# An accumulating DMA in the weight conversion, seven products for the last step of the first pair, and weights made in pairs

## The chip, the cores and the metric

The kernel runs on one NeuronCore of a Trainium2 chip, and the metric is the time of one execution on the device in microseconds (us). TensorE (PE) multiplies matrices, VectorE (DVE) and ScalarE (ACT) work element by element, GpSimd (POOL) and SyncE (SP) issue most of the DMAs. Every engine works through its own list of instructions in order; semaphores hold an instruction back until what it needs is there.

## The reference

An attention over channels and then two feed-forward layers, all in float32, with N = 6016 tokens, C = 256 channels and 2048 hidden features:

```python
qn = q / (np.linalg.norm(q, axis=1, keepdims=True) + 1e-06)   # q, k, v: (1, 6016, 256)
kn = k / (np.linalg.norm(k, axis=1, keepdims=True) + 1e-06)
s = kn.transpose(0, 2, 1) @ qn / tau                          # (256, 256)
s = s - s.max(-1, keepdims=True)
a = np.exp(s); a /= a.sum(-1, keepdims=True) + 1e-09
x = (v @ a).reshape(6016, 256)
h = x @ w_in                                                  # layer 1: 256 -> 2048
x = (h * (1.0 / (1.0 + np.exp(-1.702 * h)))) @ w_out          #          2048 -> 256
h = x @ w_in2                                                 # layer 2
x = (np.maximum(h, 0.0) + alpha * np.minimum(h, 0.0)) @ w_out2
```

The second layer's weights and alpha are inputs of their own (written w_in2, w_out2 here).

## The kernel before, in words

**Three passes for one product.** A float32 operand is held as two float32r values, hi (rounded) and lo (the rest), and a product is three matmuls: hi x hi, hi x lo, lo x hi (PASSES). The weights come as 64-bit numbers and must be turned into such pairs on the chip (class Convert, L103 to L171).

**The attention is folded into the weights.** The 256 x 256 matrix a is never applied to the tokens. For layer 1 the kernel multiplies it into w_in: for each group of 256 hidden features (j = 0 to 7) `make_w` (L480) runs 12 matmuls of 256 columns into the PSUM tile pw, and `keep_hi` on ACT (L492) and `keep_lo` on DVE (L496) store W of that j in the SBUF tile wi.

**Tiles.** Tokens go in 12 chunks (10 of 512 columns, 2 of 448), two to a pair, so 6 pairs a layer. For one pair and one j, the hidden block has 2 x 2 parts (two features groups f, two chunks c). The first pair of layer 1 forms each part directly (`direct`, L770): 4 units of two products, 24 matmuls, and beside them the 24 output matmuls (`Outs`, L699) of the j before. All other pairs use `quartet` (L792): a Winograd form with 7 products in place of 8, 21 matmuls, whose operands are sums of token blocks (T1 to T4, made by `prepare`, L542) and sums of weight blocks (S1 to S4, made by `combine`, L591). A unit is: ACT applies the activation (act, g), ACT makes its hi part (ghi), DVE its lo part (glo).

**Conversion.** A piece is 512 columns of w_in (ia[j], "inner") or w_out (ob_[j], "outer"); j = 4, 5 and 6, 7 are double pieces of 1024. Each piece is loaded by SP into one of two raw buffers (L125), scaled on ACT (scale, p, L130), and then taken through six DVE steps: shift (L133), signed (L137), power (L147), rest (L150), less (L166) and low (L169), with one ACT copy (hi, L143) between signed and less. The next raw load may start when rest has freed a buffer.

**Order.** The lists are written out by hand (manual_schedule) and filled by a small planner: after each unit `beside` (L641) first runs the put-off ACT instructions (`put_off`, in the order in which they were put off) and then as many conversion steps and background steps (`bg`) as fit into an allowance (FIRST = 2.1 us a unit in the first pair, plus up to 1.0 left over), by listed costs. `conv.need(pieces)` forces the steps until the pieces are made. In the first pair, unit 1 (the second) of each j calls `emit_w(j + 1)`, which needs ia[j + 1]; the start of j needs ob_[j - 1].

**Prologue.** PE forms the 256 x 256 product of k and q (gram) while q and k stream in; its last rows are put behind the norms (nrm), and the column factors are spread over the partitions by a small matmul (bc) that ACT copies to rq before the row scores (L458). The exponent (L463), a transpose (pt) and its hi and lo parts (eT) follow, then W of j = 0 and 1.

**End.** The last block of outputs is copied in two halves, each with its own DMA (L715 to L718).

Of the kernel before, what the change touches and what calls it, by code (L numbers as in the profile page):

```python
# [34 lines left out]
TAIL = 12  # L35
ON_VECTOR = (4, 5, 6, 8)
# [20 lines left out]
def attention_then_two_ffns(ctx: ExitStack, tc: tile.TileContext, q, k, vT, tau, w1i, w1o, w2i, w2o, alpha, outT):  # L57
# [45 lines left out]
    class Convert:  # L103
# [4 lines left out]
        most = 2 * PIECE  # L108
        pool = None

        def __init__(self, src, pair, done=None):
            self.src, self.pair, self.done = src, pair, done
            self.made = False
            self.a = src.shape[1]
            self.n = self.a * src.shape[2]
# [11 lines left out]
        def scale(self):  # L127

            self.p = self.tile("p", F32, 2)
            nc.scalar.activation(self.p, f32(self.raw[:, :, 1]), AF.Copy, scale=2.0**-112)  # L130
# [43 lines left out]
    class Converter:  # L174


        STEPS = (("shift", 0.45), ("signed", 0.7), ("power", 0.45), ("rest", 0.7), ("less", 0.7), ("low", 0.7))

        def __init__(self):
            self.todo, self.loaded, self.ready, self.open, self.at = [], [], [], None, 0  # L180

            self.ahead = False
            self.held = 0
# [13 lines left out]

        def cost(self):
            return self.time(self.open or (self.ready + self.loaded + self.todo)[0])

        def time(self, piece):
            t = self.STEPS[self.at][1]
            return 2 * t - 0.15 if piece.n > PIECE else t

        def waits(self):

            if not self.open:
# [5 lines left out]
        def needs(self):  # L213
            return [self.ready[0].scale] if self.at == 0 else [self.open.copy] if self.at == 4 else []

        def step(self):

            if self.waits():
                scalar_work()
            if not self.open:  # L220
                self.open = self.ready.pop(0)
                self.held = 1
            do, t = self.STEPS[self.at][0], self.time(self.open)
            getattr(self.open, do)()
            self.at += 1
            if do == "rest":
                self.held = 0
                self.scale()
                if self.ahead:
                    self.load()  # L230
            if self.at == len(self.STEPS):
# [11 lines left out]
        def left(self):  # L243
            return self.todo + self.loaded + self.ready + [x for x in (self.open,) if x]
# [10 lines left out]
    with tc.manual_schedule():  # L255
# [5 lines left out]
        wi_pair = {}  # L261
# [5 lines left out]
        ident = sm.tile([P, P], F32, name="ident")  # L267
        ones = sm.tile([P, P], F32, name="ones")
        ET = tuple(sm.tile([P, 2, 2, P], F32R, name=f"eT_{h}") for h in ("hi", "lo"))

        def inner(j, n=1):
            def pair():
                if j % 2 == 0:
                    t = wi_first.pop() if wi_first else wi_tiles()
# [13 lines left out]
        for made, piece, spans in ((ia, inner, ((0, 1), (1, 1), (2, 1), (3, 1), (4, 2), (6, 2))),  # L288
                                   (ob_, outer, ((0, 1), (1, 1), (2, 1), (3, 1), (4, 2), (6, 2)))):
# [3 lines left out]
        conv.todo = [ia[1], ob_[0], ia[2], ob_[1], ia[3], ob_[2], ia[4], ob_[3], ob_[4], ia[6], ob_[6]]  # L293
# [19 lines left out]
        def operand(pool=None):  # L313
# [3 lines left out]
            slot[0] += 1  # L317
            return xin[i > 3].tile([P, 2, T], F32R, tag=f"x{i}", name="x")
# [12 lines left out]
        with ExitStack() as pre:  # L331
# [96 lines left out]
            conv.steps(2)  # L428
            put_off.pop(0)()
# [13 lines left out]
            rq = sm.tile([P, C], F32, name="rq")  # L443
# [643 lines left out]
```

## Time and profile before

| | before |
|---|---|
| time, median of 3 runs | 1034.97 us (1034.52 to 1034.99) |
| profiled execution | 1034.92 us, span 1033.2 us |
| PE busy | 1027.2 us, 99% of the span |
| DVE busy | 766.1 us, 74% |
| ACT busy | 753.5 us, 73% |
| POOL busy | 31.3 us, 3% |
| granted TensorE clock, mean | 0.999 of full speed |

A profile is one execution. Its span runs from the first to the last recorded instruction; the time of the execution is 1.7 us longer. A busy share is an average over stages, so the rows below also look at single stretches. A row of the timeline begins with the start in us from the span's start and the duration; "[0.3 <-X]" says that the engine was idle for 0.3 us and that X ended it.

### The profile page before, as it was taken

To read this page: it belongs to the slowest core of one execution; us is meant where nothing else is said; L and a number is where in the kernel's file an instruction comes from. 1 tells how busy PE (TensorE), PEld (TensorE's weight loads), DVE (VectorE), ACT (ScalarE), POOL (GpSimd) and SP (SyncE) were. 2 spreads that over 40 slices of the span, in tenths; PEclk is the share of its full clock that TensorE was granted. 3 is DMA by queue.
4 is the path that set the end of the run, shared out by engine and by line. 5 is a ranking of instruction groups with operands and counts; after the bars stand their busy time and mean duration, and the time that the engine had idled before them with its cause. 6 is when DMAs were issued, how large, how long until landed. Compare 5 with 4: busy or idle time off the path is not lost.

```text
span 1033.2 us, 12543 instructions
## 1 busy us (share of the span) xinstructions
PE 1027.2 (99%) x4664; PEld 868.0 (84%) x4664; DVE 766.1 (74%) x1233; ACT 753.5 (73%) x1259; POOL 31.3 (3%) x42
## 2 busy tenths in 40 slices
PE   9999999999999999999999999999999999999998
PEld 8888888888888888888998888888888888888997
DVE  5789977878778787445637777787877787877765
ACT  6776667778777777666767777777777777867776
POOL 4400000000000000000110000000000000000000
PEclk9999999999999999999999999999999999999999
DMA  9635012125224323003543001001001000000101
GB/s 359 242 105 180 1 63 96 41 77 179 77 82 158 99 95 133 0 1 122 204 169 113 1 21 62 1 21 62 0 21 62 1 18 25 35 1 1 42 0 36
DMA packets 30605, 77.62 MB, mean 75 GB/s; under 512 B 3024, under 2 KB 7760, under 8 KB 30288
## 3 DMA queue, kind: packets, MB, share of 16 engines
q1 hardware_dynamic: 28240, 65.29, 18.1%
q0 software_dynamic: 2304, 11.54, 3.3%
q8 instruction: 36, 0.59, 0.2%
q14 instruction: 25, 0.20, 0.1%
HBM read 52.96 MB, written 23.86 MB: 74 GB/s over the span
## 4 chain that ended last, share of the span: by engine, by line
PE 99%; DMA 0%; SPq 0%; issue 0%; ACT 0%; ACTq 0%
PE ps_o L699 50%; PE ps_h L670 44%; PE gram L348 4%; PE pw L484 1%; DMA qk<-in_k 0%; SPq L368 0%; PE nrm L426 0%; PE bc L447 0%; PE pt L472 0%; ACT s L717 0%; ACTq L1083 0%
## 5 line engine op out<-in xcount | busy, mean ns | idle before, releaser
L699 PE MATMUL ps_o<-ghi,wo 128*128 128x512 f32 (+1 forms) x1536 | 562.5, 386 | 0.0
L670 PE MATMUL ps_h<-x,wi 128*128 128x512 f32 (+1 forms) x2040 | 550.7, 386 | 0.0
L670 PEld LDWEIGHTS ps_h<-x,wi 128*128 128x128 f32 x2040 | 382.2, 188 | 71.8 <-DVE wi L496 0.4
L699 PEld LDWEIGHTS ps_o<-ghi,wo 128*128 128x128 f32 x1536 | 288.6, 188 | 53.6
L699 PE MATMUL ps_o<-glo,wo 128*128 128x512 f32 (+1 forms) x768 | 296.5, 386 | 0.0
L737 DVE TENSOR_TENSOR g<-ps_h,s 128x512 f32<-128x512 f32 (+1 forms) x177 | 120.1, 678 | 94.0 <-PE ps_h L670 60.4
L766 DVE SCALAR_TENSOR_TENSOR glo<-g,sign_sb,ghi 128x512 fp32r<-128x512 f32 (+1 forms) x192 | 141.4, 737 | 55.4 <-ACT ghi L760 51.1
L803 ACT COPY s<-ps_h 128x512 f32<-128x512 f32 (+1 forms) x177 | 102.2, 577 | 104.6 <-PE ps_h L670 100.4
L768 DVE TENSOR_TENSOR glo<-g,ghi 128x512 fp32r<-128x512 f32 (+1 forms) x192 | 126.4, 677 | 67.5 <-ACT ghi L762 67.1
L699 PEld LDWEIGHTS ps_o<-glo,wo 128*128 128x128 f32 x768 | 144.3, 188 | 26.9 <-DVE glo L766 0.3
L760 ACT ACTIVATE ghi<-g,sign_sb 128x512 fp32r<-128x512 f32 (+1 forms) x192 | 137.0, 714 | 16.3 <-DVE g L756 10.9
L762 ACT CAST ghi<-g 128x512 fp32r<-128x512 f32 (+1 forms) x192 | 113.2, 611 | 3.6
L748 ACT ACTIVATE g<-ps_h 128x512 f32<-128x512 f32 (+1 forms) x112 | 65.5, 585 | 37.4 <-PE ps_h L670 36.7
L752 ACT ACTIVATE g<-g,sign_sb 128x512 f32<-128x512 f32 (+1 forms) x97 | 69.5, 717 | 29.1 <-DVE g L737 28.6
L756 DVE SCALAR_TENSOR_TENSOR g<-g,slope_sb 128x512 f32<-128x512 f32 (+1 forms) x97 | 71.6, 739 | 16.8 <-ACT g L752 16.6
L756 DVE SCALAR_TENSOR_TENSOR g<-ps_h,slope_sb,g 128x512 f32<-128x512 f32 (+1 forms) x95 | 69.7, 734 | 0.0
L814 ACT COPY ps_h<-ps_h 128x512 f32<-128x512 f32 (+1 forms) x87 | 49.0, 563 | 28.4 <-PE ps_h L670 27.8
L752 ACT ACTIVATE g<-ps_h,sign_sb 128x512 f32<-128x512 f32 (+1 forms) x95 | 64.2, 676 | 2.0 <-PE ps_h L670 0.2
L748 ACT ACTIVATE g<-g 128x512 f32<-128x512 f32 (+1 forms) x80 | 49.8, 623 | 15.5 <-DVE g L737 15.3
L348 PE MATMUL gram<-qk 128*128 128x256 f32 x156 | 34.3, 381 | 1.0 <-DMA qk<-in_k 1.0
L348 PEld LDWEIGHTS gram<-qk 128*128 128x128 f32 x156 | 29.5, 190 | 5.2 <-issue 1.4
L561 DVE TENSOR_TENSOR x<-t,x 128x512 fp32r<-128x512 f32 (+1 forms) x44 | 29.0, 672 | 0.0
(104 smaller groups left out, 504.7 us busy)
## 6 DMA issues: line engine op xcount, KB each, us to landing
wi<-w2i POOLq DMA_DIRECT2D x8, 896.0 KB, 4.9
xraw<-in_vT SPq DMA_DIRECT2D x10, 512.0 KB, 6.1
x<-ob SPq DMA_DIRECT2D x20, 256.0 KB, 2.4
xraw<-x SPq DMA_DIRECT2D x10, 512.0 KB, 3.5
out_T<-ob SPq DMA_DIRECT2D x20, 256.0 KB, 2.1
qk<-in_q SPq DMA_DIRECT2D x9, 512.0 KB, 10.2
qk<-in_k SPq DMA_DIRECT2D x9, 512.0 KB, 10.3
raw<-in_w2i SPq DMA_DIRECT2D x8, 512.0 KB, 4.1
```

The costliest lines, as they stand in the source:

```text
L348: nc.tensor.matmul(gram[m][:, :C], tiles[i][:, 1, r, m * P:(m + 1) * P], tiles[i][:, 0, r, :], start=(t == 0), stop=(t == R - 1))
L670: nc.tensor.matmul(ps[:, :n], WI[:, wq, a, blk], x[:, b, :n], start=(start and i == 0), stop=(stop and i == 2), skip_group_check=True)
L699: nc.tensor.matmul(acc_ps[c][d][:, :n], WO[:, j, a, f, d * P:(d + 1) * P], (hi, lo)[b][:, :n], start=(start and i == 0), stop=(stop and i ...
L737: nc.vector.tensor_tensor(self.src, ps[:, :self.n], s[:, :self.n], ALU.add)
L748: nc.scalar.activation(self.g, self.src, AF.Gelu_apprx_sigmoid)
L752: nc.scalar.activation(self.g, self.src, AF.Copy, scale=sign_sb[:, self.f])
L756: nc.vector.scalar_tensor_tensor(self.g, self.src, slope_sb[:, self.f], self.g, ALU.mult, ALU.max)
L760: nc.scalar.activation(self.hi, self.g, AF.Copy, scale=sign_sb[:, self.f])
L762: nc.scalar.copy(self.hi, self.g)
L766: nc.vector.scalar_tensor_tensor(self.lo, self.g, sign_sb[:, self.f], f32(self.hi), ALU.mult, ALU.subtract)
L768: nc.vector.tensor_tensor(self.lo, self.g, f32(self.hi), ALU.subtract)
L803: nc.scalar.copy(s[:, :n], ps[:, :n])
```

## The change

All of it lies in the prologue, the first pair of layer 1 and its weights, except for the last output copy.

- Pieces of the first layer are all 512 columns wide. Those with j > 1 (inner) and j > 0 (outer) are "added": their steps are shift, settle, signed, power, rest. After rest, `sent` issues a DMA on POOL's queue that adds top into p in SBUF. The ACT copy to hi is put off at the rest of the next piece (`ask`), and `split` (lo = p - hi, one DVE operation) is done in the settle step of a later piece. p has three buffers and top two.
- The last j of the first pair (j = 7, STRASSEN) goes through `quartet`; its sums of tokens are made in j = 4 to 6 and its sums of weights in j = 5 and 6. The two chunks of the next pair are loaded at j = 6 instead of 3.
- W of j = 4, 5 and of 6, 7 is made by `emit_pair`: 12 matmuls of 512 columns for two j.
- In the prologue the first half of gram is copied to SBUF early, the row scores read bc from PSUM, rq is copied later and without tau (which goes into the row factors), and two rows of gram instead of one follow the first transpose. ident, ones and rq share one tile, which with G serves as scratch for the quartet of j = 7. The operand slots are taken in another order.
- The last output block is one copy and one DMA.

```diff
         def signed(self):
-            self.top = self.tile("top", F32, 1)
+            self.top = self.tile("top", F32, 2 if Convert.deep else 1)
             nc.vector.scalar_tensor_tensor(u32(self.top), self.raw[:, :, 1], 0x80000000, u32(self.p),
                                            ALU.bitwise_and, ALU.bitwise_or)
-            self.hi, self.lo = self.pair()
-            put_off.append(self.copy)
+            if not self.added:
+                self.hi, self.lo = self.pair()
+                put_off.append(self.copy)
 
...
         def copy(self):
+            if self.added:
+                self.hi, self.lo = self.pair()
+                self.top = self.p
             nc.scalar.copy(self.hi, self.like(self.top))
...
+
+        def sent(self):
+            nc.gpsimd.dma_start(out=self.p, in_=self.top, accum_op=ALU.add)
+
+        def split(self):
+            nc.vector.tensor_tensor(self.lo, self.like(self.p), f32(self.hi), ALU.subtract)
+            self.made = True
...
         STEPS = (("shift", 0.45), ("signed", 0.7), ("power", 0.45), ("rest", 0.7), ("less", 0.7), ("low", 0.7))
+        ADDED = (("shift", 0.45), ("settle", 0.7), ("signed", 0.7), ("power", 0.45), ("rest", 0.7))
...
+            do, t = self.list(piece)[self.at]
+            return 0 if do == "settle" and not self.landed() else t
+
+        def landed(self):
+            return self.flying and self.flying[0].asked
+
+        def ask(self):
+            if self.flying and not self.flying[0].asked:
+                self.flying[0].asked = True
+                put_off.append(self.flying[0].copy)
...
             if not self.open:
                 self.open = self.ready.pop(0)
                 self.held = 1
-            do, t = self.STEPS[self.at][0], self.time(self.open)
-            getattr(self.open, do)()
+            steps = self.list(self.open)
+            do, t = steps[self.at][0], self.time(self.open)
+            if do != "settle":
+                getattr(self.open, do)()
+            elif self.landed():
+                self.settle()
             self.at += 1
             if do == "rest":
                 self.held = 0
                 self.scale()
+                if self.open.added:
+                    self.ask()
                 if self.ahead:
                     self.load()
-            if self.at == len(self.STEPS):
+            if self.at == len(steps):
+                if self.open.added:
+                    self.open.sent()
+                    self.flying.append(self.open)
                 self.open, self.at = None, 0
             return t
...
-            return Convert(w1i.rearrange("p (a n) -> p a n", a=2)[:, :, j * C:(j + n) * C], pair)
+            return Convert(w1i.rearrange("p (a n) -> p a n", a=2)[:, :, j * C:(j + n) * C], pair, added=j > 1)
...
-            return Convert(w1o[:, j * PIECE:(j + n) * PIECE].rearrange("p (a n) -> p a n", a=1), pair)
+            return Convert(w1o[:, j * PIECE:(j + n) * PIECE].rearrange("p (a n) -> p a n", a=1), pair, added=j > 0)
...
-        conv.todo = [ia[1], ob_[0], ia[2], ob_[1], ia[3], ob_[2], ia[4], ob_[3], ob_[4], ia[6], ob_[6]]
+        conv.todo = [ia[1], ob_[0], ia[2], ob_[1], ia[3], ob_[2], ia[4], ia[5], ob_[3], ob_[4], ia[6], ia[7], ob_[5], ob_[6], ob_[7]]
...
             conv.steps(2)
+            nc.scalar.copy(G[:, 0], gram[0][:, :C])
             put_off.pop(0)()
             conv.steps(2)
...
-            nc.scalar.activation(rq, bc[:, :C], AF.Copy, scale=tau_sb)
-            low(0, 0)
-            high(1, 0)
+            nc.vector.tensor_scalar(rr[:, 2:4], rr[:, 2:4], tau_sb, None, ALU.mult)
...
-            nc.vector.tensor_tensor_reduce(G[:, m], gram[m][:, :C], rq, rr[:, 2 + m:3 + m], -3e38, ALU.mult, ALU.max,
+            nc.vector.tensor_tensor_reduce(G[:, m], *((gram[1][:, :C], rq) if m else (G[:, 0], bc[:, :C])), rr[:, 2 + m:3 + m], -3e38, ALU.mult, ALU.max,
                                            mx[:, m:m + 1])
...
         scores(0)
         exponent(0)
-        emit_gram(range(R - TAIL + 4, R - 1), (1,))
+        nc.scalar.copy(rq, bc[:, :C])
+        high(1, 0)
+        low(0, 0)
+        emit_gram(range(R - TAIL + 4, R - 2), (1,))
         conv.steps(1)
...
+        def emit_pair(j):
+
+            conv.need([ia[j], ia[j + 1]])
+            for m in range(2):
+                pw = psh.tile([P, T], F32, tag="h", name="pw")
+                for n, (a, b, i) in enumerate((a, b, i) for a, b in PASSES for i in range(2)):
+                    nc.tensor.matmul(pw, ET[a][:, m, i], wi_whole[j][b][:, i], start=(n == 0), stop=(n == 5))
+                hi, lo = (WI[:, j:j + 2, h, 2 * m:2 * m + 2] for h in range(2))
+                src = pw.rearrange("p (j a b) -> p j a b", j=2, a=2)
+                nc.scalar.activation(hi, src, AF.Copy, scale=rs[:, m:m + 1])
+                nc.vector.scalar_tensor_tensor(lo, src, rs[:, m:m + 1], f32(hi), ALU.mult, ALU.subtract)
...
-                        for at in (slice(0, n // 2), slice(n // 2, n)):
-                            ob = sp.tile([P, T], F32, tag="s", name="s", bufs=3)
-                            nc.scalar.copy(ob[:, :n // 2], acc_ps[c][d][:, at])
-                            nc.sync.dma_start(dst[:, at], ob[:, :n // 2])
+                        ob = sp.tile([P, T], F32, tag="s", name="s", bufs=3)
+                        nc.scalar.copy(ob[:, :n], acc_ps[c][d][:, :n])
+                        nc.sync.dma_start(dst, ob[:, :n])
...
-                beside(FIRST, convert=True)
+                beside(FIRST, convert=not own_first[0])
...
             def copy(ps):
+                if narrow:
+                    s = small.pop(0)
+                    small.append(s)
+                    nc.scalar.copy(s, ps)
+                    return s
...
             def mid_way(i):
-                if j < NQ - 1 and i == 1:
+                if j < 3 and i == 1:
                     if j == 0:
                         conv.need([ob_[0]])
                     emit_w(j + 1)
+                if j == 3 and i == 1:
+                    emit_pair(4)
+                if j == 5 and i == 1:
+                    emit_pair(6)
+                    own_first[0] = True
+                    combining_of(7)
...
+                if j == 4 and i == 0:
+                    sums0.extend(prepare(0, 0))
+                    bg.extend(sums0)
+                if j == 6 and i == 0:
+                    own_first[0] = False
+                    finish(sums0)
+                    for c in range(2):
+                        load_tokens(0, 2 + c)
+                if j == 6 and i == 2:
+                    pair1.extend(prepare(0, 1))
+                    bg.extend(pair1[0][:3])
+                    combining_of(0)
+                    bg.extend(pair1[0][3:])
+
+            if j < STRASSEN:
+                outs = direct(j, outs, mid_way)
+                continue
+            finish(combined[j])
+            rest = [x for x in pair1[0] if x in bg]
+            for x in rest:
+                bg.remove(x)
+            first(rest + pair1[1])
+            outs = quartet(0, 0, j, outs, carry)
         conv.need(ob_.values())
-        finish(list(bg))
+        finish(combined[0] + pair1[0])
+        steps_late = [x for x in pair1[1] if x in bg]
...
+                if i == 0:
+                    fresh = [n for n in ((1, 2) if j == 0 else (j + 2,)) if n < STRASSEN]
+                    combined.update({n: combine_wi(n) for n in fresh})
+                    first(sum((combined[n] for n in fresh), []))
```

## Rows read from the trace of the kernel before

**Rows 1.** The page: busy time of the engines, and the chain that ended last.
```profile
PE 1027.2 (99%) x4664; PEld 868.0 (84%) x4664; DVE 766.1 (74%) x1233; ACT 753.5 (73%) x1259; POOL 31.3 (3%) x42
...
PE 99%; DMA 0%; SPq 0%; issue 0%; ACT 0%; ACTq 0%
```

**Rows 2.** The chain in order of time: start us, us, what.
```profile
63.29 1.44 PE pw L484 x12
75.64 1.43 PE pw L484 x12
...
213.68 1.36 PE ps_h L670 x6
```

**Rows 3.** Busy time by stretch: us, then each engine's busy us, clock, DMA.
```profile
60.00:90.00 30.00, 30.00 (x151) 25.51 (x150) 28.33 (x47) 20.68 (x36) 0.00 (x0) 1.00 0.39 123
```

**Rows 4.** Timeline of DVE, third inner piece: start, us, line, operation.
```profile
59.75 0.69 DVE L150 SCALAR_TENSOR_TENSOR p<-raw,p 128x512 f32<-128x512 uint32 x1
...
61.75 0.69 DVE L169 TENSOR_TENSOR wi_lo<-top,p 128x512 fp32r<-128x512 f32 x1
62.36 0.42 DVE L133 TENSOR_SCALAR p<-p 128x512 uint32<-128x512 uint32 x1
```

**Rows 5.** Timeline of PE, W of j = 2.
```profile
63.36 0.40 PE L484 MATMUL pw<-wi_lo,eT_hi 128*128 128x256 f32 x2
```

**Rows 6.** Raw loads: one issue, its us to landing, then all from 30 to 110.
```profile
60.51 0.55 SPq L125 DMA_DIRECT2D raw<-in_w1i  x1
...
raw<-in_w1i SPq DMA_DIRECT2D x1, 512.0 KB, 4.3
...
DMA to landing us min/median/max: 3.5/4.8/7.2
```

**Rows 7.** Timeline of ACT beside the third inner piece.
```profile
63.54 0.62 ACT L143 CAST wo<-top 128x512 fp32r<-128x512 f32 x1 [1.90 <-DVE top L137]
...
65.21 0.67 ACT L130 ACTIVATE p<-raw 128x512 f32<-128x512 f32 x1
```

**Rows 8.** DMA issues: queue, count, KB each, median us to landing.
```profile
x<-ob SPq DMA_DIRECT2D x20, 256.0 KB, 2.4
...
qk<-in_k SPq DMA_DIRECT2D x9, 512.0 KB, 10.3
...
wo<-w2o POOLq DMA_DIRECT2D x8, 512.0 KB, 5.5
```

**Rows 9.** Timeline of ACT and PE where the second pair begins.
```profile
128.23 1.13 ACT L557 CAST x<-t 128x512 fp32r<-128x512 f32 x2
...
142.16 0.60 ACT L748 ACTIVATE g<-ps_h 128x512 f32<-128x512 f32 x1 [1.47 <-PE ps_h L670]
142.79 0.62 ACT L762 CAST ghi<-g 128x512 fp32r<-128x512 f32 x1
143.52 0.57 ACT L814 COPY ps_h<-ps_h 128x512 f32<-128x512 f32 x1
...
145.36 0.84 PE L670 MATMUL ps_h<-x,wi 128*128 128x512 f32 x3
```

**Rows 10.** Timeline of ACT and DVE in the prologue.
```profile
44.81 0.47 ACT L448 ACTIVATE rq<-bc,tau_sb 128x256 f32<-128x256 f32 x1 [0.54 <-PE bc L447]
...
45.31 0.48 DVE L458 CUSTOM_DVE_ANT_0 G<-gram,rq,rr 128x256 f32<-128x256 f32 x1
...
48.05 0.37 ACT L477 CAST eT_hi<-pt 128x256 fp32r<-128x256 f32 x1 [0.28 <-PE pt L472]
```

**Rows 11.** The end: timeline of ACT and SP, then issues with us to landing.
```profile
1029.34 0.59 ACT L717 COPY s<-ps_o 128x224 f32<-128x224 f32 x2
1029.71 0.90 SPq L718 DMA_DIRECT2D out_T<-s  x2
...
out_T<-ob SPq DMA_DIRECT2D x3, 224.0 KB, 2.0
...
out_T<-s SPq DMA_DIRECT2D x2, 112.0 KB, 1.9
```

More of the change, by code (lines that the diff above doesn't have):

```diff
@@ L35 @@
 TAIL = 12
+STRASSEN = 7
 ON_VECTOR = (4, 5, 6, 8)
@@ L103, in attention_then_two_ffns, with __init__ @@
     class Convert:
-        most = 2 * PIECE
+        most = PIECE
         pool = None
-        def __init__(self, src, pair, done=None):
-            self.src, self.pair, self.done = src, pair, done
+        deep = True
+        def __init__(self, src, pair, done=None, added=False):
+            self.src, self.pair, self.done, self.added = src, pair, done, added
+            self.asked = False
             self.made = False
@@ L196, in scale, with next, list @@
                 self.ready.append(x)
+        def next(self):
+            return self.open or (self.ready + self.loaded + self.todo + [None])[0]
+        def list(self, piece):
+            return self.ADDED if piece and piece.added else self.STEPS
         def cost(self):
-            return self.time(self.open or (self.ready + self.loaded + self.todo)[0])
+            return self.time(self.next())
         def time(self, piece):
-            t = self.STEPS[self.at][1]
-            return 2 * t - 0.15 if piece.n > PIECE else t
+            if not piece:
+                return 0.7
+            do, t = self.list(piece)[self.at]
[6 more added lines that the diff above has]
+                put_off.append(self.flying[0].copy)
         def waits(self):
+            if not self.next():
+                self.ask()
+                return self.flying[0].copy in put_off
             if not self.open:
@@ L213, in needs, with settle @@
         def needs(self):
-            return [self.ready[0].scale] if self.at == 0 else [self.open.copy] if self.at == 4 else []
+            if not self.next():
+                return [self.flying[0].copy]
+            if self.at == 0:
+                return [self.ready[0].scale]
+            if self.open.added:
+                return [self.flying[0].copy] if self.at == 1 and self.landed() else []
+            return [self.open.copy] if self.at == 4 else []
+        def settle(self):
+            self.flying.pop(0).split()
         def step(self):
@@ L219, in step @@
                 scalar_work()
+            if not self.next():
+                self.settle()
+                return 0.7
             if not self.open:
@@ L284, in pair @@
                 return tuple(WO[:, j:j + n, h].rearrange("p q a b -> p q (a b)") if n > 1 else flat(WO[:, j, h]) for h in range(2))
-            return Convert(w1o[:, j * PIECE:(j + n) * PIECE].rearrange("p (a n) -> p a n", a=1), pair)
+            return Convert(w1o[:, j * PIECE:(j + n) * PIECE].rearrange("p (a n) -> p a n", a=1), pair, added=j > 0)
         ia, ob_ = {}, {}
-        for made, piece, spans in ((ia, inner, ((0, 1), (1, 1), (2, 1), (3, 1), (4, 2), (6, 2))),
-                                   (ob_, outer, ((0, 1), (1, 1), (2, 1), (3, 1), (4, 2), (6, 2)))):
+        for made, piece, spans in ((ia, inner, [(j, 1) for j in range(NQ)]),
+                                   (ob_, outer, [(j, 1) for j in range(NQ)])):
             for j, n in spans:
@@ L588, in prepare @@
             ]
+            if (l, p) == (0, 0):
+                return [early[i] for i in (2, 3, 6, 7)] + [late[i] for i in (0, 1, 2, 4, 5)]
             return early, late
@@ L770, in direct @@
         def direct(j, outs, mid_way):
-            ops = operands[0, 0]
+            ops = blocks
             units = []
@@ L913, in attention_then_two_ffns, with combining_of @@
         scalar_work()
-        del raws[0, 0], raws[0, 1]
-        outs = None
+        operands[0, 0] = {"B11": blocks[1, 0], "B12": blocks[1, 1], "B21": blocks[0, 0], "B22": blocks[0, 1]}
+        small = [flat(G), mixed]
+        sums0, pair1 = [], []
+        outs, carry = None, []
         steps_late = []
-        combined = []
+        combined = {}
+        def combining_of(n):
+            combined[n] = combine_wi(n)
+            bg.extend(combined[n])
+        own_first = [False]
         for j in range(NQ):
@@ L926, in mid_way @@
                     emit_w(j + 1)
+                if j == 3 and i == 1:
[4 more added lines that the diff above has]
+                    combining_of(7)
                 if j == 2 and i == 0:
                     nc.sync.dma_start(alpha_sb, alpha)
-                if j == 3 and i < 2:
-                    load_tokens(0, 2 + i)
-                if j == 5 and i == 0:
-                    early, late = prepare(0, 1)
-                    bg.extend(early + late)
-                    for n in range(AHEAD):
-                        combined.append(combine_wi(n))
-                        bg.extend(combined[n])
-            outs = direct(j, outs, mid_way)
+                if j == 4 and i == 0:
[20 more added lines that the diff above has]
+            outs = quartet(0, 0, j, outs, carry)
         conv.need(ob_.values())
-        finish(list(bg))
+        finish(combined[0] + pair1[0])
+        steps_late = [x for x in pair1[1] if x in bg]
         smx.close()
@@ L1014, in attention_then_two_ffns @@
                     first(rest + nxt_late)
-                if i == 0 and j + AHEAD < NQ:
-                    combined.append(combine_wi(j + AHEAD))
-                    first(combined[-1])
+                if i == 0:
+                    fresh = [n for n in ((1, 2) if j == 0 else (j + 2,)) if n < STRASSEN]
+                    combined.update({n: combine_wi(n) for n in fresh})
+                    first(sum((combined[n] for n in fresh), []))
                 outs = quartet(l, p, j, outs, carry)
```

28 lines of the change are left out of this document (17 added, 11 removed).

## The prediction

> **What bounds the kernel now.** I read the page's busy times first, then the chain that ended last: TensorE (PE) is busy 99% of the span and the chain is PE for 99% of it [rows 1]. The reader is to see that no other engine is a bound on average (VectorE, DVE, 74%; ScalarE, ACT, 73%). The second view is the chain in order of time. Eight groups of column blocks (j = 0 to 7) make up the first pair of token chunks. In it one j costs 24 products, 24 output matmuls and one weight block W: six matmuls of 512 columns take 1.36 us, that is 0.227 each, and the twelve 256-column matmuls of W (tile pw) take 1.44 [rows 2]. 48 x 0.227 + 1.44 = 12.32, and the pw of two successive j start 12.35 apart (63.29, 75.64). So PE has no gap to give back inside the first pair: the time falls only by PE work that goes away, and every new wait of PE is paid in full. The third view, busy time by stretch, shows where such a wait can come from: from 60 to 90 us DVE is busy 28.33 of 30 us [rows 3]; there the weights are converted just ahead of their use.
>
> **The change part by part.**
>
> *PE work removed.* The last j of the first pair goes from 24 products to 7 x 3 = 21: 3 x 0.227 = 0.68 less. W for j = 4, 5 and for 6, 7 is made as twelve 512-column matmuls per pair: 12 x 0.227 = 2.72 for 2 x 1.44 = 2.88, so 0.16 less, twice [rows 2]. Together 1.00 us less, all of it on the path.
>
> *The conversion of the third inner piece (W of j = 2).* This is the term that decides. Before, the piece needs on DVE shift, signed, power, rest, less and low; its rest starts at 59.75 and takes 0.69, its low (wi_lo) is done at 61.75 + 0.69 = 62.44, and the first matmul that reads wi_lo starts at 63.36: under a microsecond to spare [rows 4, 5]. After, the piece is not finished by its own steps. Its sum is sent through the accumulating DMA at the rest (60.44); its copy to wi_hi is put off until the next piece's rest, and behind the scale of the piece after that, because the planner puts off that scale first; its split (wi_lo) stands on DVE behind that later piece's shift. Following the planner's allowance of 2.1 us a unit and its listed costs (0.45, 0.7, 0.7, 0.45, 0.7), I get: unit 1 of j = 0 does signed, power, rest; unit 2 all of ob1; unit 3 has ACT do scale(ia3), copy(ia2) and DVE shift(ia3), split(ia2). Only then, at unit 1 of j = 1, is pw issued. So wi_lo waits for the raw data of ia3. That load is issued at 60.51, when the rest has freed one of two raw buffers, as before, and landed 4.3 us later; raw loads here take 3.5 to 7.2, median 4.8 [rows 6]. I take 4.8, since the accumulating DMA now shares the DMA engines with this load. Then: landing 65.31; scale on ACT, the copy 0.51 behind it (two casts take 1.13, one 0.62 [rows 9]) at 65.82, done 66.44; meanwhile the shift (0.42) ends at 66.4; split 0.69 to 67.13, and 0.05 to PE: 67.2 against 63.36. PE waits 3.8 us. Bounds: landing after 3.5 gives 2.5, after 7.2 gives 6.2. ACT and DVE hold other units' work behind these instructions (the next act, glo of unit 3), but PE itself stands still meanwhile, so that adds nothing. In the before trace ACT has this scale at 65.21 and copied the next piece (wo) at 63.54 [rows 7], off PE's path, because wi_lo no longer hung on them.
>
> *The accumulating DMA itself* is not in the trace. It moves 256 KB. The nearest rows: 2.4 us for 256 KB from SBUF by SP's queue, 5.5 for 512 KB by POOL's, 10.3 for the most crowded loads [rows 8]. It must land by 65.8 so as not to lengthen the sum, 5.3 us after sending; I take that it does, at 4 to 5 (nearer to POOL's row, since it is issued there and reads two operands). At 10.3 the copy would start at 70.8, the split end at 72.1 and the wait be 8.8.
> The Trainium skill (SBUF — State Buffer, section "SBUF: two separate sides") has a rule that speaks against this change: a DMA issued from GpSimd has its descriptors written by GpSimd, which is shut out while DVE runs an operation in a mode using two ports, so the transfer starves. The trace has POOL's copies landing after 5.5 us beside a DVE busy 74% over the span, so there it cost a few us at most; no run shows it under a DVE busy 94%. By the rule the time would come out as in the third rival below.
>
> *DVE work.* Thirteen of the sixteen pieces lose one operation (less and low become split): 13 x 0.69 = 9 us less, and the second halves of the four double pieces pay their fixed cost again. That helps later: after W of j = 2 the planner's split of each W piece stands two or more units ahead of its pw, so I count 0 for the later j. What hides the longer way is a unit of 2.72 us (12 x 0.227) or more; if loads took 7 us each, that cover would be gone and another 1 to 3 us would come at j = 3 or 4. The sums for the seven products (nine steps of 0.7) and one combine go into j = 4 to 6, where conversion ends: 0.
>
> *The start of the seven products.* In the last direct j, unit 2 of j = 6 runs six steps for the second pair and puts off five ACT copies (B11, B21, T1, combined sums, T2; the planner's 2.1 plus 1.0 carried over just covers them). They go to ACT after the unit 3 output and before the bank copy that the first quartet needs. At the same place before (start of the second pair) ACT ends ghi at 142.79 + 0.62, does the bank copy at 143.52 for 0.57, and PE's third product starts at 145.36 [rows 9]. With five casts of 0.51 from 143.30 the copy runs from 145.85 to 146.42: PE waits 1.1 us. Bounds: 0 if the casts find ACT early, 1.5 if one of them waits.
>
> *Prologue.* The row scores (45.31) no longer wait for rq on ACT (44.81) but for PE's broadcast, at which rq starts: some 0.5 earlier; in exchange rq and one cast now stand behind the exponent, in front of eT_hi (48.05), where ACT had 0.28 idle [rows 10]: 0.37 + 0.51 moved in, 0.5 and 0.28 given, and a tau multiplication and a copy of gram are new. I take +0.3; bounds -0.3 (the present waits of PE there gone) and +0.6.
>
> *End.* One copy and one DMA in place of two. Before, the first copy starts at 1029.34, the two issues run from 1029.71 to 1030.61, so the second starts near 1030.16 and lands 1.9 later, 1032.06. After: copy 0.53, issue at 1029.9, landing 2.0 later, 1031.9 [rows 11]. -0.15; bounds -0.4 and +0.2.
>
> *Sum.* -1.00 + 3.8 + 1.1 + 0.3 - 0.15 = +4.05. The profiled execution took 1034.92 (span 1033.2), the median of the runs is 1034.97: no correction. 1034.92 + 4.05 = 1039.0.
>
> **The rivals.**
> - *The third inner piece is in time* (not slower). Mechanism: split(ia2) reaches PE before 63.36, at pw of j = 2. For that the copy must not stand behind the load of ia3; it decides at a landing of 61.5, one microsecond after issue. For it: DVE sheds work, and the wait now has slack of 0.9. Against: no raw load lands under 3.5, and the planner's order. Time: -1.00 + 0.3 - 0.15 and half of the second wait, 0.55: 1034.6; with neither wait and the prologue's best, 1033.5.
> - *Only one of the two new waits*: without the second, 1037.9; with the load at 3.5 too, 1036.6. For it: ACT is idle near 140 us (1.47 ahead of an act [rows 9]).
> - *The accumulating DMA is slow* (starved descriptors or two-operand reads), landing like the most crowded loads: the first wait 8.8 in place of 3.8, 1044.0; every later copy would hold ACT too, adding up to a few us. For it: thirteen such DMAs in the busiest DVE stretch. Against: POOL's row, 5.5 for twice the bytes [rows 8].
> - *The seven products save nothing*, because the added copies eat the 0.68: that is the second wait already counted.
>
> **How the numbers follow.** The forecast with both waits: 0.5, own range 1037 to 1041. Only one wait or both short: 0.24, 1035.5 to 1038. In time: 0.13, 1033.5 to 1035.5. Slow DMA: 0.13, 1041 to 1047. The range 1034.8 to 1044.0 leaves out some 0.1 on either side. About 0.2% (2.07 us) is what a measurement of this kernel can tell from no change. Faster than 1032.9 would take all gains at their best and more than the bounds above give: 0.05. Slower than 1037.04: the forecast nearly whole, the slow DMA and part of the one-wait case: 0.67. Within: 0.28.
>
> **What would show each step.** In the trace after: 27 fewer matmuls (3 products; 24 in place of 48 for W of j = 4 to 7), as far as the records are complete; PE idle before the first pw with wi_lo, at 63 to 67 us, ended by the ACT copy or DVE split behind a raw load; ACT idle before scale(ia3); a second PE wait near 146 to 150, ended by the ACT bank copy; no other idle of PE until the end. Wrong would be: PE dense through 70 us (then the planner's order was misread); ACT waiting for the accumulating DMA rather than the raw load (then its latency is the price); PE waits at later pw.

## The result and the profile after

The changed kernel takes 1043.77 us (median of 5 runs, 1042.47 to 1043.98) against 1034.97: ratio 1.0083, 95% interval 1.0071 to 1.0094. It is slower by 8.8 us; the forecast was 1039.0, slower, with a range up to 1044.0. The profiled execution took 1043.98 us, its span is 1042.1.

The page after, the rows that answer to [rows 1]: busy time of the engines and the chain that ended last, by engine.

```profile
span 1042.1 us, 12578 instructions
...
PE 1031.0 (99%) x4637; PEld 869.1 (83%) x4637; DVE 766.6 (74%) x1252; ACT 758.6 (73%) x1270; POOL 43.1 (4%) x55
...
PE 93%; ACT 1%; DMA 1%; issue 0%; DVE 0%
```

The reader is to see two things. PE runs 27 matmuls fewer (4637 for 4664) and is yet busy 3.8 us longer: some of them ran slower. And the chain, which was PE for 99% of the span, now is for 93%: other engines and a DMA have come onto the path. Where, the view of PE's waits says (what it waited for, us in total, times, longest):

```profile
PE pw L540 <- ACT wi_hi L150: 3.8, 1, 3.8
PE pw L540 <- ACT eT_hi L533: 1.5, 1, 1.5
...
PE ps_h L743 <- ACT ps_h L892: 1.0, 1, 1.0
```

To turn waits into a sum, the same work is looked up in both traces and its starts are compared. The rows of PE's timeline before at the first W, the first product and the W of j = 2 (start us, us):

```profile
48.47 0.51 PE L484 MATMUL pw<-wi_hi,eT_hi 128*128 128x256 f32 x2
...
50.07 1.26 PE L670 MATMUL ps_h<-x,wi 128*128 128x512 f32 x4
...
63.12 0.40 PE L484 MATMUL pw<-wi_hi,eT_hi 128*128 128x256 f32 x2
```

The chain before, where the last output matmuls end:

```profile
1023.55 5.77 PE ps_o L699 x27
```

The same timeline after, and behind it the same chain:

```profile
50.17 0.51 PE L540 MATMUL pw<-wi_hi,eT_hi 128*128 128x256 f32 x2 [1.53 <-ACT eT_hi L533]
...
52.06 1.24 PE L743 MATMUL ps_h<-x,wi 128*128 128x512 f32 x4 [0.19 <-ACT wi L548]
...
69.09 0.80 PE L540 MATMUL pw<-wi_hi,eT_hi 128*128 128x256 f32 x2 [3.81 <-ACT wi_hi L150]
```

```profile
69.09 3.23 PE pw L540 x12
84.78 1.44 PE pw L540 x12
...
1032.87 5.74 PE ps_o L772 x27
```

| Place | before | after | behind by | added there | forecast |
|---|---|---|---|---|---|
| first product | 50.07 | 52.06 | 1.99 | +1.99 | +0.3 |
| pw of j = 2, its wait | 63.12 | 69.09 | 5.97 | +3.98 | +3.8 |
| pw of j = 3 [rows 2] | 75.64 | 84.78 | 9.14 | +3.17 | 0 |
| end of the last output matmuls | 1029.32 | 1038.61 | 9.29 | +0.15 | -1.00 + 1.1 |
| span | 1033.2 | 1042.1 | 8.9 | -0.4 | -0.15 |

The third line stands for no wait at all. Busy time by stretch (us, then PE, PEld, DVE, ACT, POOL busy with counts, PEclk, DMA share, GB/s) shows what it is:

```profile
60.00:65.00 5.00, 5.00 (x24) 3.99 (x22) 4.68 (x9) 2.90 (x6) 1.03 (x1) 1.00 0.23 30
65.00:69.00 4.00, 0.28 (x2) 0.00 (x0) 1.30 (x3) 1.24 (x3) 0.87 (x1) 0.95 1.01 273
69.00:71.00 2.00, 1.91 (x7) 1.69 (x8) 1.90 (x4) 1.94 (x5) 0.00 (x0) 0.50 0.75 165
...
73.00:75.00 2.00, 2.00 (x6) 1.61 (x5) 1.29 (x4) 1.55 (x3) 0.17 (x1) 0.50 0.65 84
...
75.50:77.00 1.50, 1.50 (x8) 1.23 (x7) 1.43 (x4) 1.03 (x2) 0.00 (x0) 1.00 1.09 276
```

PE stood nearly still from 65 to 69 us; from 69 to 75 its granted clock was 0.50, the 1.2 GHz level, and from 75.5 on 1.00 again. Some 6.4 us at half speed do the work of 3.2: the 3.17. The same table has a second thing to see, in the last two columns of its second row: while PE waits, the 16 DMA engines are full (share 1.01).

Who waits for what at j = 2 stands in the timeline of DVE, ACT, SP and POOL after (the rows that answer to [rows 4 to 7]):

```profile
61.72 0.69 DVE L157 SCALAR_TENSOR_TENSOR p<-raw,p 128x512 f32<-128x512 uint32 x1
...
62.48 0.55 SPq L128 DMA_DIRECT2D raw<-in_w1i  x1
62.75 1.03 POOL L160 DMA_DIRECT2D p<-top  x1 [22.81 <-DVE p L157]
...
67.23 0.66 ACT L133 ACTIVATE p<-raw 128x512 f32<-128x512 f32 x1 [4.26 <-DMA raw<-in_w1i]
...
68.42 0.62 ACT L150 CAST wi_hi<-p 128x512 fp32r<-128x512 f32 x1 [0.53 <-DMA p<-top]
69.07 0.69 DVE L163 TENSOR_TENSOR wi_lo<-p,wi_hi 128x512 fp32r<-128x512 f32 x1 [0.72 <-ACT wi_hi L150]
```

The order is the one forecast: the scale of ia3 (67.23) stands ahead of ia2's copy (68.42) and waits 4.26 us for its raw load. But the copy behind it was idle another 0.53 us for the accumulating DMA. Two transfers that run at the same time end the wait nearly together; the issue rows (KB each, median us to landing) price the new one:

```profile
raw<-in_w1i SPq DMA_DIRECT2D x8, 512.0 KB, 4.6
...
p<-top POOLq DMA_DIRECT2D x13, 256.0 KB, 5.0
```

### The profile page after: what moved, and what is told of

It reads as the page before. It is cut to its first block, busy times and chain, and to the rows that moved or that the text cites. A ratio compares the mean times of both kernels' runs of the same rounds, so it can differ in the third digit from the quotient of the medians.

```text
span 1042.1 us, 12578 instructions
## 1 busy us (share of the span) xinstructions
PE 1031.0 (99%) x4637; PEld 869.1 (83%) x4637; DVE 766.6 (74%) x1252; ACT 758.6 (73%) x1270; POOL 43.1 (4%) x55
## 4 chain that ended last, share of the span: by engine, by line
PE 93%; ACT 1%; DMA 1%; issue 0%; DVE 0%
PE ps_o L772 49%; PE ps_h L743 43%; DMA p<-top 1%; PE pw L687 1%; PE pw L540 1%; ACT x L616 0%; ACT g L820 0%; ACT wi L548 0%; ACT L986 0%; ACT ghi L834 0%; DVE p L157 0%; DVE top L140 0%; ACT wi_hi L150 0%; ACT s L789 0%; ACT x L383 0%
## 5 line engine op out<-in xcount | busy, mean ns | idle before, releaser
L620 DVE TENSOR_TENSOR x<-t,x 128x512 fp32r<-128x512 f32 (+1 forms) x48 | 31.7, 671 | 0.0
```

## The experiments

The time of before was 1034.90 to 1035.02 beside all of them. A "new wait" is one of PE.

**The prologue.** PE's 1.53 us there is ended by eT_hi. ACT's timeline in the changed kernel:

```profile
48.67 0.62 ACT L383 CAST x<-xraw 128x512 fp32r<-128x512 f32 x1 [1.53 <-PE gram L406]
...
49.77 0.35 ACT L533 CAST eT_hi<-pt 128x256 fp32r<-128x256 f32 x1
```

A cast of a token block (`high(0, 1)`) stands ahead of eT_hi in ACT's list and waits for the last gram matmuls. The change's new slot order gives that block slot 4, the first in the pool opened over the released q and k buffers, which those matmuls still read. Theory: with slots 0 and 4 exchanged the wait goes.

```
             if slot[0] <= 8:
                 i = (2, 1, 4, 0, 3, 5, 6, 7)[i]
+            i = {0: 4, 4: 0}.get(i, i)
```

> The changed kernel with the SBUF places of operand slots 0 and 4 swapped, so that the third token block is written in the first pool, which shares no memory with the q and k buffers, and the fourth in the second. Theory: in the changed kernel ACT's cast of the third block sat idle 1.53 us until the last gram matmul (48.67 us), because its new place lies where those matmuls still read, and eT_hi and the first pw stood behind it; so the first pw comes 1.5 us earlier and the time falls from 1043.8 to about 1042.3. Rival: the later pw comes from rq and one cast moved behind the exponent, as the prediction had it (+0.3); then the time stays within 0.3 us of 1043.8.

Measured 1041.49 us (ratio 1.0062, 1.0050 to 1.0075), 2.3 less. PE's timeline of this run, the first W and the first product:

```profile
48.22 0.51 PE L541 MATMUL pw<-wi_hi,eT_hi 128*128 128x256 f32 x2
...
49.81 1.71 PE L744 MATMUL ps_h<-x,wi 128*128 128x512 f32 x6
```

No idle time stands before either, and the wait at j = 2 is still 3.77. The first product is 2.25 us earlier than in the changed kernel and 0.26 earlier than in the kernel before. So this line alone makes the whole loss of the prologue, and what else the change moved there cost PE nothing.

**The half clock.** Theory: it follows from PE's standing still. Rival: it belongs to what runs at 69 to 75 us. 18 spare matmuls, whose sum is discarded, keep PE at work during the wait:

```
+            for _ in range(18 if j == 2 else 0):
+                nc.tensor.matmul(pw[:, :P], ones, ones, start=True, stop=True)
```

> The changed kernel with 18 spare float32 matmuls of 128 columns (3.8 us at the full clock) issued into the bank of pw just before the pw of j = 2, where PE sat idle 4 us; they take the place of idleness and are overwritten. Theory: the half clock from 69 to 75 us follows from PE's idle stretch, so with PE busy pw starts at the same 69 us but runs at the full clock, and the time falls by 2.5 to 3.1, to about 1041. Rival: the slow stretch has another cause (SBUF or DMA traffic, the late wi_lo); then the time stays within 0.5 of 1043.8.

Measured 1041.17 us (1.0058, 1.0044 to 1.0072), 2.6 less with more work on PE. Busy time by stretch of this run:

```profile
65.00:69.00 4.00, 4.00 (x38) 3.98 (x36) 1.20 (x4) 1.45 (x3) 0.87 (x1) 1.00 1.04 264
...
71.00:73.00 2.00, 2.00 (x11) 1.62 (x10) 1.84 (x4) 0.72 (x3) 0.85 (x1) 1.00 0.01 2
```

The same DMA load, the same instructions, and the clock stays at 1.00. The theory holds.

**What ends the wait at j = 2.** My step said the raw load of ia3. If so, a third raw buffer, which lets that load start earlier, ends it; if the accumulating DMA does by itself, it doesn't.

```
-            self.raw = self.tile("raw", U32, RAWS, 2)
+            self.raw = self.tile("raw", U32, 3 if Convert.deep else RAWS, 2)
```

(and the planner's limit of pieces in hand raised from 2 to 3 for the first layer)

> The changed kernel with three raw buffers instead of two from the first pair's loop on, so that the load of the piece behind the third inner one is issued some 5 us earlier. By the prediction's step (wi_hi stands behind the scale of that piece, which waits for its load) the wait before the pw of j = 2 falls by 3 us or more and with it the half clock: 1038 to 1040. Rival: the accumulating DMA, which landed 5.6 us after its issue, 0.5 us later than that scale ended, ends the wait by itself; then the pw starts 0 to 1.5 us earlier, only as far as the DMA is quicker without a load beside it, and the time stays within 1042 to 1044.

Measured 1041.93 us (1.0067, 1.0054 to 1.0080). The chain ahead of PE's wait, and PE's timeline there:

```profile
62.73 4.63 DMA p<-top
```

```profile
68.05 0.50 PE L541 MATMUL pw<-wi_hi,eT_hi 128*128 128x256 f32 x2 [2.86 <-ACT wi_hi L150]
```

The load of ia3 is out of the way and 2.86 of 3.81 us are left: the accumulating DMA alone is enough for them, as the rival had it. Is that the price of the addition, or of the queue? Two runs replace it by a plain copy of the same 256 KB, which leaves out the addition of the lower part: one on the same queue, one on SP's.

```
-            nc.gpsimd.dma_start(out=self.p, in_=self.top, accum_op=ALU.add)
+            nc.gpsimd.dma_start(out=self.p, in_=self.top)      # the first run
+            nc.sync.dma_start(out=self.p, in_=self.top)        # the second
```

> The changed kernel with a plain copy in place of the accumulating one, from the same queue (POOL) and with the same bytes; it leaves out the addition of the low part. Theory: the addition costs, because the destination is read too: landing falls from a median of 5.0 us to 4 or less, PE waits at most 0.6 us less before the pw of j = 2 (then the load behind it ends the wait), 1043 to 1043.8. Rival: POOL's queue and the load beside it set the time, the landing stays within 0.3 of 5.0 and the time at 1043.8.

> As e7_pool, but the plain copy is issued by SP's queue. Theory: it lands after 2.2 to 3 us like SP's other 256 KB copies from SBUF; the wait before the pw of j = 2 is then ended by the scale that waits for the next raw load, as the prediction had it: PE idle 3.2 to 3.4 instead of 3.8, the half clock shorter or the same, 1041.5 to 1043.3. Rival: the landing stays at 4 us or more, because 128 rows of 2 KB beside a load of 512 KB cost that on any queue.

Measured 1041.93 us (1.0066, 1.0052 to 1.0080) and 1042.17 (1.0070, 1.0056 to 1.0083). The first landed between what theory and rival had said and was faster than either; of the second the rival had the landing right. The issue rows of the first, then of the second:

```profile
p<-top POOLq DMA_DIRECT2D x13, 256.0 KB, 4.3
```

```profile
p<-top SPq DMA_DIRECT2D x13, 256.0 KB, 4.6
```

Medians of 4.3 and 4.6 us stand against 5.0 with the addition. But with the addition and three raw buffers the median was 4.4, so these medians do not price it. What does is a single transfer that ran alone: in the changed kernel the issue at 117.23 us, in the run with the copy on POOL's queue the one at 114.41. Their issue rows, and between them the busy time by stretch of the first:

```profile
p<-top POOLq DMA_DIRECT2D x1, 256.0 KB, 3.3
```

```profile
117.23:120.53 3.30, 3.30 (x16) 2.74 (x15) 3.27 (x7) 2.40 (x5) 0.88 (x1) 1.00 0.46 79
```

```profile
p<-top POOLq DMA_DIRECT2D x1, 256.0 KB, 2.3
```

79 GB/s for 3.3 us are the 256 KB themselves: nothing else moved, and nothing did beside the other one (114 GB/s for 2.3 us). So the addition costs 1.0 us when the transfer is alone, by one transfer of each kind. The other twelve in the changed kernel had loads beside them and took 4.3 to 6.3 us, the one that PE waited for 5.6. That the loads make the difference is read from these transfers; no run took the loads away. With the copy faster, the raw load ended the wait, at 3.08 and 3.29 us: either of the two transfers by itself holds PE for about 3 us. The Trainium skill (SBUF — State Buffer, section "SBUF: two separate sides") let one expect that a transfer issued from GpSimd starves while DVE runs an operation in a mode that uses two ports. Here the one at 117.23 us landed in 3.3 although DVE was busy for 3.27 of the 3.30 us, and the copy on SP's queue took no less than that on POOL's, so the rule does not explain this case.

**Later pieces.** I had counted 0 for them. Giving ia2 the old steps takes away the wait at j = 2 and shows whether that holds when PE is on time.

```
-            return Convert(w1i..., pair, added=j > 1)
+            return Convert(w1i..., pair, added=j > 2)
```

> The changed kernel with the third inner piece (W of j = 2) converted by the six old steps, the other twelve still by the accumulating DMA. Theory: PE's wait of 4.0 us before the pw of j = 2 and the half clock behind it (3.1 us by the records) both go, nothing takes their place since every later piece is two units ahead: 1043.8 - 7.1 = 1036.7. Rival: conversion is late altogether, and the wait only moves to the pw of j = 3 or 4; then 1039 or more.

Measured 1039.57 us (1.0047, 1.0035 to 1.0060), 2.9 more than expected. The wait at j = 2 and the half clock are gone, and in their place stands a new one at the pw of the pair j = 4, 5, shown here by the chain and then by PE's timeline:

```profile
70.06 11.53 DMA p<-top x2
...
87.23 4.38 DMA p<-top
```

```profile
92.30 0.73 PE L687 MATMUL pw<-wi_hi,eT_hi 128*128 128x512 f32 x2 [2.10 <-ACT wi_hi L150]
```

That is the rival's outcome. The copy of a piece waits for its DMA, later steps for that copy and for a raw buffer, and so the accumulating DMAs, one behind the other, set the pace up to this pair. In the changed kernel PE, 9 us late by then, did not see it.

The next run puts the repairs together: slots exchanged, ia2 by the old steps, three raw buffers, and in the unit before the seven products only two put-off casts ahead of the bank copy:

```
-                beside(FIRST, convert=not own_first[0])
+                beside(FIRST, convert=not own_first[0], most=2 if (j, i) == (6, 3) else None)
```

> The changed kernel with four edits: operand slots 0 and 4 swapped, the third inner piece converted by the old steps, three raw buffers in the first pair's loop, and at most two of the five put-off casts before the bank copy that begins the seven products. Theory: these take away every new wait of PE that the traces show (1.5 to 1.9 in the prologue, 4.0 and the half clock at W of j = 2, the 2.1 that e2_plain2 then had at W of j = 4 and 5, 1.2 at the seven products), and what is left is the 1.0 us of PE work removed: 1033.7 to 1034.3, below the kernel before. Rival: the pieces are paced by the accumulating DMA itself (3.3 to 6.3 us each, one after the other with the loads), so that PE still waits 1 to 2 us before W of j = 4 and 5: 1035 to 1036.

Measured 1039.19 us (1.0040, 1.0027 to 1.0054). The waits in the prologue and at the seven products are gone, yet PE's timeline has two others:

```profile
71.99 0.50 PE L774 MATMUL ps_o<-ghi,wo 128*128 128x512 f32 x1 [1.08 <-ACT wo L150]
...
91.84 1.22 PE L689 MATMUL pw<-wi_hi,eT_hi 128*128 128x512 f32 x2 [2.18 <-ACT wi_hi L150]
```

One sits at a w_out piece (ob1), one again at the pair j = 4; ia3, which went through the DMA too, was in time. The rival had the second place right, but not the time (1035 to 1036): it had no term for ob1 nor for the half clock, which came back behind the 2.18 us (pw took 4.57 us in place of 2.73).

The opposite: no accumulating DMA at all, all pieces of 512 columns by the old steps, slots and casts repaired.

> The changed kernel without any accumulating DMA (all pieces of 512 columns by the six old steps, hi placed at the copy), with slots 0 and 4 swapped and at most two put-off casts before the bank copy. Theory: DVE has 9 us more to do in the first pair, but it has 10 to 20% idle there and no piece waits for a DMA in the middle: 1033.7 to 1034.5, as good as with the accumulating DMA mended, which then buys nothing. Rival: DVE needs the relief, since the sums for the seven products add some 6 us in the same stretch; then PE waits 1 us or more for a W or for the seven products: 1035 or more.

Measured 1044.06 us (1.0085, 1.0071 to 1.0098). PE's timeline:

```profile
133.66 0.73 PE L747 MATMUL ps_h<-x,wi 128*128 128x512 f32 x2 [1.17 <-ACT wi L676]
135.54 0.50 PE L747 MATMUL ps_h<-x,wi 128*128 128x512 f32 x1 [1.15 <-DVE wi L673]
149.12 1.65 PE L747 MATMUL ps_h<-x,wi 128*128 128x512 f32 x3 [3.54 <-ACT wi L676]
```

PE is dense to 130 us, then waits for the sums of the seven products, and the half clock follows (mean 0.66 from 145 to 155 us). From 90 to 130 us DVE was busy 37.95 of 40 us here, 34.66 in the changed kernel. This fits the rival: the seven products put work on DVE which the accumulating DMA takes off it, and the two halves of the change belong together. It is not shown, since the planner's order of sums and conversions was not varied in this version.

**A version between the two.** Old steps for the pieces wanted first (ia2, ob1, ia3), accumulating DMAs from ob2 and ia4 on, W of the pair j = 4 one unit later, and the repairs above; once with three raw buffers, once with two.

```
-                if j == 3 and i == 1:
+                if j == 3 and i == 2:
                     emit_pair(4)
...   added=j > 3 for the inner pieces, j > 1 for the outer
```

> The kernel after with the prologue's slot order mended, three raw buffers, the fourth beside() of j=6 held to two put-off casts, the pieces that are wanted first (ia2, ob1, ia3) converted by the old steps, accumulating DMAs only from ob2 and ia4 on, and the first pair of W's blocks (j=4, 5) made one unit later in j=3. If the loss is the accumulating DMA's time in front of pieces that are wanted at once, no wait of PE over 0.5 us is left between 48 and 150 us, the clock stays at 1.00 there, and the time is that of before less the 1.0 us of PE work and 0.3 us at the end: 1033.2 to 1034.2 us, faster than before. If later accumulated pieces are paced by the DMA too (rival), a wait of 1 to 2.5 us stands at the pair of j=4 or at W's last outputs (j=1 to 3) and the time is 1035.5 to 1038. If VectorE has too little room for the three pieces of old steps, PE waits at the pw of j=3 (0.5 to 2 us): 1034.5 to 1036.

> As e10_mix, but with the two raw buffers of the kernel after. If the third raw buffer does nothing once the first pieces are made in the old way, the same time as e10_mix within 0.3 us. If the raw loads set the pace (rival), a wait of PE ended by a scale behind a raw load stands between 60 and 100 us and the time is 1 to 3 us above that of e10_mix.

Measured 1036.60 us (1.0016, 1.0008 to 1.0025) and 1036.55 (1.0018, 1.0008 to 1.0027): the third raw buffer does nothing, and waits are left, as the rival of the first run had it. In that run:

```profile
PE ps_o L774 <- DVE wo L163: 1.3, 1, 1.3
...
PE pw L689 <- ACT wi_hi L150: 0.6, 1, 0.6
```

The first is ob5's split, which the planner ran behind the sums of the seven products. Letting conversion go first for one unit more:

```
-                    own_first[0] = True
                     combining_of(7)
+                if j == 5 and i == 2:
+                    own_first[0] = True
```

> As e10_mix (1036.6 us, idle of PE 0.60 us at the pw of the pair j=4 and 1.25 us at W's last outputs of j=5), but the sums of the seven products take precedence over the conversions one unit later in j=5, so that the sixth last-layer piece (ob5) is split before them. If that order made the 1.25 us, the idle time at 124 us is gone and the time falls by 1.0 to 1.25 us, to 1035.3 to 1035.6: not yet below before, since the wait at the pair of j=4 stays. If VectorE has no room for both (rival, as in e6), the wait moves behind to the next piece or to the start of the seven products (130 to 150 us) and the time stays at 1036.3 to 1037.

Measured 1034.74 us beside 1035.02 of before (ratio 0.9997, 0.9988 to 1.0006): level with before, 9 us below the change and 0.6 below the expected range. One wait is left, at the pair j = 4, behind ia5's DMA, here in the chain and in PE's timeline:

```profile
84.79 6.00 DMA p<-top
...
91.49 3.29 PE pw L689 x12
```

```profile
91.49 0.73 PE L689 MATMUL pw<-wi_hi,eT_hi 128*128 128x512 f32 x2 [0.98 <-ACT wi_hi L150]
```

Its price is 0.98 and, as wi_lo is late too, 3.29 - 2.73 in pw itself: 1.5 us, the gain that is missing. The last run gives ia4 the old steps as well, to free the way for ia5.

> As e12_own (1034.74 us against 1035.02 of before), but ia4 by the old steps too, so that the first accumulating DMA of W's pairs is that of ia5, with one fewer in flight beside it and no split of ob2 ahead of it on VectorE. If the remaining wait at the pair of j=4 (1.0 us, and pw 3.29 instead of 2.73 us) comes from ia5's accumulating DMA, issued at 84.79 and 6.0 us long, it goes or shrinks below 0.3 us and the time falls to 1033.3 to 1034.0, faster than before. If the DMA is as long and issued no earlier (rival), the wait stays at 1 us and the time at 1034.5 to 1035; if VectorE has no room for the sixth piece of old steps, a wait at W's last outputs of j=2 (ob2's split) takes its place and the time is 1034.5 to 1036.

Measured 1037.52 us (1.0025, 1.0015 to 1.0036). PE's timeline:

```profile
84.72 0.50 PE L774 MATMUL ps_o<-ghi,wo 128*128 128x512 f32 x1 [1.42 <-ACT wo L150]
...
86.50 0.50 PE L774 MATMUL ps_o<-ghi,wo 128*128 128x512 f32 x1 [1.04 <-DVE wo L163]
```

The wait at the pair is gone (pw takes 2.73 again), but ob2's copy and split were put behind ia4's and ia5's steps and come too late. The last rival named the place, but its time (1034.5 to 1036) was too low, and its reason is doubtful: without any accumulating DMA, DVE made all pieces in time here. The planner's order, which asks for ob2's copy only when the next accumulated piece is at its rest, is the likelier reason; no run tested it. No version run here beats the kernel before.

## Why the prediction was right, and where not

The direction and the place were right; the sum was 4.85 us short (+4.05 against +8.9 in the span). That the time still lies inside the range is luck: the range reached 1044.0 for the sake of a rival that did not occur. By its steps:

- *PE work removed*, -1.00, and *the start of the seven products*, +1.1. Together +0.15 was measured for +0.1. The wait there is 1.02 us, ended by the bank copy behind the five put-off casts, as worked out.
- *The third inner piece*, +3.8, measured +3.98. The raw load was issued 1.97 us later than before (the prologue) and its scale ran at 67.23; the sum with that shift gives 65.31 + 1.97 = 67.28. What the step had wrong is that the load sets the end by itself: the *accumulating DMA*, allowed 5.3 us, took 5.64 in the chain and ended the wait 0.53 behind the scale, and with the load out of the way it still cost 2.86.
- *No term for the clock.* "PE itself stands still meanwhile, so that adds nothing" was said of the other engines' work; what the standing still does to PE itself got no term, and that is the step that failed: it cost another 3.17 us at 1.2 GHz, and the run with spare matmuls got 2.6 of it back. It is the largest part of the error.
- *Prologue*, +0.3 with bounds -0.3 and +0.6, measured +1.99: the second failed step. I priced the instructions that move on ACT, and the new slot order, which is part of the same change, at nothing. With the slots exchanged the prologue was 0.26 us ahead of before, so the order is all of it. The order decides whose memory a tile takes over, and so whom its first writer waits for.
- *"0 for the later j."* It held in the changed kernel for a reason that the step did not have: the cover was PE's own lateness. With ia2 in time, 2.10 us came up at the pair j = 4.
- *End*, -0.15: about -0.4 in the span, with one copy and one DMA as described.
- The *rival* of a slow accumulating DMA gave 1044.0, close to the measured 1043.77, but not by its mechanism: the DMAs took a median of 5.0 us and 6.3 at most, not 10. "Seven products save nothing" holds for the change as it stands, not in itself: with the casts limited that wait goes, and in the mended version that is level with before the gains and a remaining wait of 1.5 us balance.

## What to carry to other kernels

Where the bounding engine has no gaps, a step that goes through a DMA needs its slack counted from the consumer back, piece by piece: here such a relief did harm at pieces converted just ahead of use, and a piece with units in hand could still be late (ia5, 0.98 us). Price a wait of TensorE with what its clock does afterwards, and look at which freed memory each tile is placed in. And a wait that hides another is not a cover: take the first away in thought and go through the rest again.

## What the runs showed of the hardware

The granted clock after a wait of PE, by each run's own rows: after 3.81 us idle it was 0.50 for some 6 us; after 2.86 us (three raw buffers) it was 0.51 from 70 to 73 us; after 2.18 us (repairs together) pw took 4.57 us in place of 2.73. At 2.10 us (ia2 by the old steps) and at 0.98 us no stretch behind the wait was below 1.00. Busy time by stretch of the second and third:

```profile
70.00:73.00 3.00, 3.00 (x10) 2.41 (x9) 2.46 (x5) 1.76 (x5) 0.85 (x1) 0.51 0.33 43
```

```profile
90.00:95.00 5.00, 3.16 (x8) 2.44 (x8) 3.14 (x6) 3.04 (x6) 0.10 (x1) 0.68 0.72 173
```

Waits of nearly one length went both ways; what decides between them stays open. In one of the five executions with ia2 by the old steps the mean clock was 0.998 and the time 1041.29 us, against 0.999 or more and at most 1040.03 us in the others, so the 2.10 us may have cost the clock there too.

A 256 KB transfer within SBUF took 3.3 us with the addition and 2.3 us as a plain copy when nothing else moved, and medians of 4.3 to 5.1 us over the runs, on either queue, most of them beside raw loads. The Trainium skill (DMA: Bandwidth & Descriptors, section "Anatomy of one DMA — SWDGE (gpsimd) path") gives 2.0 us and the bytes at 436 GB/s, an estimate of 2.6 us. The plain copy alone is near it; the accumulating one, alone, took 0.7 us more.
